# Attention and a max-out feed-forward layer on one core: the first q and k on other queues, another order in batch 0, and another way to sum the last 64 queries

## The chip, the cores and the metric

The kernel runs on one core of a Trainium2 chip. The metric is the time of one execution on the device in microseconds (us); a kernel is run several times and the median is given. A core has five engines that run at the same time and wait for one another through semaphores: PE (matrix multiplication; its weight loads are listed as PEld), DVE (vector), ACT (scalar functions such as exp), POOL (general purpose) and SP (issues transfers). ACT and POOL issue transfers as well. SBUF is the working memory with 128 partitions; PSUM is the small memory that PE writes to and that DVE and ACT empty. Each engine runs its instructions in the order of the program.

## The reference

Attention on 8 batches of 12 heads, 448 queries and keys, 64 values a head, with 1 added to the softmax's sum ("off by one"), and then a feed-forward layer whose hidden value is the maximum of three products:

```
scores = scale * q @ k.T                       # 8 x 12 heads, 448 x 448, d = 64
m = max(scores);  e = exp(scores - m)
attn = e / (sum(e) + exp(-m) + 1e-09)
x = (attn @ v) as tokens x 768                 # 3584 tokens, 12 heads x 64
h = max(x @ w1, x @ w2, x @ w3)                # 768 x 768 each
out = h @ w_out                                # 3584 x 768, fp32
```

Inputs and output are fp32. The kernel computes its products in fp16 and takes exp without subtracting the maximum, so the denominator is the sum of exponentials plus 1.

## The kernel before, in words

**Groups.** Four heads of one batch make a group: 24 groups, three a batch. A pair (`pr` 0 or 1) is two heads of a group. A group's q and k come as `ld_q` and `ld_k`, v as `ld_v`, all cast to fp16 by POOL's transfers (`load_qk`, L113; `load_v`, L123 and L126; weights `load_weight`, L137). There are four buffers of each kind. Of groups 0 and 1 q and k are loaded pair by pair.

**Scores.** q and k must lie with the head's 64 values on partitions. For groups 0 to 6 PE transposes them into PSUM tiles `trT` (`transpose_pe`, L205, for groups 0 to 2; `transpose_once`, L221, for 3 to 6) and ACT or DVE copies them to `KT` and `QT` (`evac`, L180 or L182); later groups use transposing transfers on SP (L233), and POOL completes `QT` (`shift_q`, L241). `scores` (L296) multiplies 64x64 blocks of k with all query columns into PSUM tiles `stp`; ACT takes the exponential into `e` (L316). The blocks are worked in seven units, 0 to 6.

**Sums of values.** For each pair `av_tail` (L336) adds the block of keys that both heads share a tile for, with 64*64 matmuls, and `av_main` (L353) the rest, with 128*128 matmuls: the weights are 128 queries of `e`, the moving data are 64 values and a column of constants that gives the sum of exponentials. Both write a tile `avp` of the same PSUM pool (`ps_s`, 3 buffers) as `stp`. 448 queries are worked as four windows of 128, of which the last holds only 64 that count. DVE then adds the 1 (`rb`, L363), takes the reciprocal (L366) and multiplies (`xn`, L369). `xn` is transposed to `xT`, by PE for batches 0 and 1 (`x_transpose_pe`, L396; `x_transpose_all`, L409), then by SP's transfers (L419).

**Feed-forward.** `up_piece` (L436) multiplies one of the three weights with `xT` into a PSUM tile `p_i`: six matmuls of 448 columns a piece, or twelve where a batch's columns are cut into even and odd queries. DVE copies the first weight's product to `hT` (L445) and takes the maximum for the others (L447). `out_piece` (L460) multiplies with `w_out` into `op_ps`, six matmuls, DVE scales it into `o_sb` (L467), SP stores it (L477). `p_i`, `op_ps` and most transposes share the PSUM pool `ps_b`, which has two buffers.

**Order.** The order is written out by hand. The program's first part takes groups 0 to 2 (batch 0) in two passes, first three of seven query columns ("O"), then four ("E"), so that PE has work while loads arrive; `warm` runs matmuls on zeros. Then the loop `for i in range(3, NI)` makes three visits a group: the scores of two, two and three units, in the first two visits the sums of the group before, and then `fill`, which takes pieces of feed-forward work from a list until a credit of columns is used up. In a visit PE thus runs scores (8 or 12 matmuls), a sum (16 + 24), and usually two or three pieces.

Window `w` of block `n` starts in `e` at

```
n * S + ((192, 320, 0, 128) if n % 2 == 0 else (0, 128, 256, 384))[w]
```

Of the kernel before, what the change touches and what calls it, by code (L numbers as in the profile page):

```python
# [21 lines left out]
def kernel(  # L22
# [33 lines left out]
    PE_QK = 7  # L56
    NF = 3
    PE_X = 2
    NEB = 2
    NV = 3  # L60

    tabs = list(get_activation_tables(nc.m.arch).keys())
    act_set = tabs.index("natural_log_exp_and_others")
    nc.scalar.add_instruction(
        mybir.InstLoadActFuncSet(
            name=nc.get_next_instruction_name(),
            act_func_set_id=act_set,
            ins=[],
            outs=[],
        )  # L70
    )

    cpool = ctx.enter_context(tc.tile_pool(name="const", bufs=1))
    att_pool = ctx.enter_context(tc.tile_pool(name="att", bufs=3))
    small = ctx.enter_context(tc.tile_pool(name="small", bufs=3))
    xn_pool = ctx.enter_context(tc.tile_pool(name="xn", bufs=3))
    xt_pool = ctx.enter_context(tc.tile_pool(name="xt", bufs=3))
    ht_pool = ctx.enter_context(tc.tile_pool(name="ht", bufs=2))
    out_pool = ctx.enter_context(tc.tile_pool(name="outp", bufs=3))

    ps_s = ctx.enter_context(tc.tile_pool(name="ps_s", bufs=3, space=bass.MemoryType.PSUM))
    ps_b = ctx.enter_context(tc.tile_pool(name="ps_b", bufs=2, space=bass.MemoryType.PSUM))
# [56 lines left out]

    wz = cpool.tile([128, 512], MMDT, name="wz")  # L140
    nc.vector.memset(wz, 0.0)
    load_qk(0, "kq", (0, 1))
    load_qk(0, "kq", (1, 2))
    ident16 = cpool.tile([128, 128], MMDT, name="ident16")
    make_identity(nc, ident16)
    load_qk(1, "kq", (0, 1))
    load_qk(1, "kq", (1, 2))
    load_v(0)
    load_qk(2)
    load_v(1)  # L150
# [8 lines left out]
    for j in range(NEB):  # L159
        nc.vector.memset(e_buf[j][:, NB * S : NB * S + HP], 0.0)  # L160
        blk = e_buf[j][:, 0 : NB * S].rearrange("p (n s) -> p n s", s=2 * S)
        nc.vector.memset(blk[:, :, NO : NO + HP], 0.0)

    def warm(n, cols=512):
        ps = ps_b.tile([128, 512], FP32, tag="b", name="warm")
# [152 lines left out]
    def e_col(n, w):  # L318

        return n * S + ((192, 320, 0, 128) if n % 2 == 0 else (0, 128, 256, 384))[w]  # L320
# [21 lines left out]
                        skip_group_check=True,  # L342
                    )

    def av_main(i, ej, pr, ws=(0, 1, 2, 3)):
        eF, vx = e_buf[ej], v_buf[i % NV]
        ps = avs.pop((i, pr))
        nw = len(ws)
        for hh in range(2):
            for j, w in enumerate(ws):  # L350
                for c, x in enumerate((X1, X3, X2)):
                    o = e_col(where[pr, hh, x], w)
                    nc.tensor.matmul(  # L353
                        out=ps[:, hh, j * D1 : (j + 1) * D1],
                        lhsT=eF[:, o : o + 128],
                        rhs=vx[:, 2 * pr + hh, (x[0]), 0:D1],
                        start=False,
                        stop=(c == 2),
                        skip_group_check=True,
                    )  # L360
        acc = ps[:, :, 0 : nw * D1].rearrange("p h (j d) -> p h j d", d=D1)
        rb = small.tile([P, 2, 4], FP32, tag="rb", name="rb")
        nc.vector.tensor_scalar(  # L363
            out=rb[:, :, 0:nw], in0=acc[:, :, :, D], scalar1=1.0 / LAMBDA, scalar2=None, op0=ALU.add
        )
        nc.vector.reciprocal(out=rb[:, :, 0:nw], in_=rb[:, :, 0:nw])  # L366
        if i not in xn:
            xn[i] = xn_pool.tile([P, NP, 4, 2, D], MMDT, tag="xn", name="xn")
        nc.vector.tensor_tensor(  # L369
            out=xn[i][:, pr, ws[0] : ws[0] + nw].rearrange("p j h d -> p h j d"),  # L370
            in0=acc[:, :, :, 0:D],
            in1=rb[:, :, 0:nw].unsqueeze(3).to_broadcast([P, 2, nw, D]),
            op=ALU.mult,
        )

    def prep_v(i, eng):
        t = raw[i]["v"]
# [198 lines left out]
    for n in (4, 5):  # L576
        ej, part, g, pp, pg = n % NEB, "E", n - 3, "E", n - 4
        scores(g, ej, (0, 1), part)
        scores(g, ej, (2, 3), part)
        av(pg, 1 - ej, 0, pp)  # L580
        if n == 4:
            transpose_once(3, "q", AC)
        else:
            x_transpose_pe(0, "E")
        fill(STEP)
        scores(g, ej, (4, 5), part)
        scores(g, ej, (6,), part)
        av(pg, 1 - ej, 1, pp)
        if n == 4:
            transpose_once(3, "k", AC)  # L590
        fill(STEP)
        if n == 4:
            shift_q(3, PL)
            load_v(4)
            load_qk(5)
            load_weight(3)


    visits = ((0, 1), (2, 3), (4, 5, 6))
# [18 lines left out]
    for i in range(3, NI):  # L618
        ej, pj = (i + 1) % NEB, i % NEB
        first = i == 3  # L620
        if PE_QK <= i + 2 < NI:
            transpose_dma(i + 2)
        if first:
            load_v(i + 2)
        for vi, units in enumerate(visits):
            n = 3 * i + vi
            scores(i, ej, units)
            if i == 4 and vi == 0:
                prep_v(i, DV)
            if vi < 2:  # L630
                av(i - 1, pj, vi, "E" if first else "EO")
            if vi == 1 and i > 3 * PE_X:
                x_transpose_dma(i - 1)
            if n in adds:
                add_batch(adds[n])
            per = STEP if first and vi < 2 else share(n)
            if vi == 0 and first:
                x_transpose_pe(1, "E")
            if vi == 2 and first:
                x_transpose_pe(i - 1, "E")  # L640
                fill(per / 2)
# [61 lines left out]
```

## Time and profile before

The median of 11 runs is 343.56 us (342.79 to 344.65).

| | |
|---|---|
| profiled execution, its own time | 344.66 us |
| span from its first to its last instruction | 342.9 us |
| PE busy | 329.2 us (96%) |
| DVE busy | 187.5 us (55%) |
| ACT busy | 151.4 us (44%) |
| POOL busy | 148.3 us (43%) |
| granted PE clock | 0.999 |

The page gives busy times, the chain of work that ended last (followed back from the last instruction, at each step to what released it), groups of instructions by line with their mean duration and the idle time before them, and transfers. In a line of a group or of the timeline, `out<-in` are the program's names, sizes are partitions x elements, `xN` is how many instructions it stands for, and square brackets tell how long the engine stood idle before and what it waited for. Starts are in us from the span's start. A line of the waits gives us in total, how many times, and the longest one.

### The profile page before, as it was taken

To read this page: it belongs to the slowest core of one execution; us is meant where nothing else is said; L and a number is where in the kernel's file an instruction comes from. 1 tells how busy PE (TensorE), PEld (TensorE's weight loads), DVE (VectorE), ACT (ScalarE), POOL (GpSimd) and SP (SyncE) were. 2 spreads that over 40 slices of the span, in tenths; PEclk is the share of its full clock that TensorE was granted. 3 is DMA by queue.
4 is the path that set the end of the run, shared out by engine and by line. 5 is a ranking of instruction groups with operands and counts; after the bars stand their busy time and mean duration, and the time that the engine had idled before them with its cause. 6 is when DMAs were issued, how large, how long until landed. Compare 5 with 4: busy or idle time off the path is not lost.

```text
span 342.9 us, 9827 instructions
## 1 busy us (share of the span) xinstructions
PE 329.2 (96%) x4175; PEld 199.1 (58%) x4175; DVE 187.5 (55%) x407; ACT 151.4 (44%) x181; POOL 148.3 (43%) x265
## 2 busy tenths in 40 slices
PE   7788899999999999999999999999999999999994
PEld 3556788766556555556556655556556655565552
DVE  3463566655555556555556556555556555565553
ACT  2757667664554444453444444543444444200000
POOL 8495688593772445373372465272454000000000
PEclk9999999999999999999999999999999999999999
DMA  7999999799899999969989999979993550124006
GB/s 86 192 164 187 204 207 201 108 162 202 154 122 120 162 222 142 170 74 236 137 111 94 187 215 124 114 128 203 160 117 46 124 125 3 31 67 106 0 15 169
DMA packets 84844, 46.19 MB, mean 135 GB/s; under 512 B 53312, under 2 KB 81344, under 8 KB 84800
## 3 DMA queue, kind: packets, MB, share of 16 engines
q0 software_dynamic: 29440, 22.03, 50.5%
q1 hardware_dynamic: 55120, 23.37, 38.0%
q8 instruction: 32, 0.52, 0.6%
q10 hardware_dynamic: 240, 0.16, 0.2%
q14 instruction: 12, 0.10, 0.1%
HBM read 44.04 MB, written 11.01 MB: 161 GB/s over the span
## 4 chain that ended last, share of the span: by engine, by line
PE 86%; DMA 8%; POOL 3%; issue 1%; DVE 0%; POOLq 0%
PE p_i L436 46%; PE op_ps L460 16%; PE avp L353 11%; PE stp L296 10%; DMA w<-in_moe_w_dram 4%; DMA ld_v<-in_v_dram 2%; PE avp L336 2%; DMA ld_q<-in_q_dram 2%; POOL w L137 1%; POOL ld_k L113 1%; POOL ld_q L113 1%; PE trT L221 1%; PE xtp L409 0%; POOL vx L379 0%; POOL vt L382 0%
## 5 line engine op out<-in xcount | busy, mean ns | idle before, releaser
L316 ACT ACTIVATE e<-stp 128x896 f16<-128x896 f32 (+4 forms) x171 | 144.2, 903 | 138.7 <-PE stp L296 138.6
L436 PE MATMUL p_i<-xT,w 128*128 128x448 f16 (+2 forms) x972 | 173.8, 332 | 2.9 <-DMA w<-in_moe_w_dram 2.8
L436 PEld LDWEIGHTS <-w 128*128 128x128 f16 x972 | 89.8, 98 | 70.8 <-issue 4.8
L241 POOL COPY QT<-QT 64x384 f16<-64x384 f16 (+1 forms) x84 | 46.7, 556 | 97.5 <-DMA QT<-ld_q 74.1
L447 DVE TENSOR_TENSOR hT<-hT,p_i 128x448 f16<-128x448 f16 (+2 forms) x96 | 59.7, 621 | 48.2 <-PE p_i L436 48.0
L460 PE MATMUL op_ps<-w,hT 128*128 128x384 f16 (+2 forms) x342 | 58.1, 323 | 0.0
L296 PE MATMUL stp<-QT,KT 64*64 64x448 f16 (+2 forms) x756 | 47.6, 338 | 2.4 <-DVE QT L182 2.0
L353 PE MATMUL avp<-vx,e 128*128 128x65 f16 x1152 | 45.4, 193 | 0.0
L460 PEld LDWEIGHTS <-hT 128*128 128x128 f16 x342 | 32.1, 98 | 22.7 <-issue 2.0
L467 DVE TENSOR_SCALAR o_sb<-op_ps 128x384 f32<-128x384 f32 (+2 forms) x57 | 31.2, 549 | 24.0 <-PE op_ps L460 22.3
L445 DVE CAST hT<-p_i 128x448 f16<-128x448 f32 (+2 forms) x48 | 30.0, 625 | 22.3 <-PE p_i L436 22.2
L353 PEld LDWEIGHTS <-e 128*128 128x128 f16 x1152 | 38.8, 97 | 2.3
L369 DVE TENSOR_TENSOR xn<-avp,rb 128x512 f16<-128x512 f32 (+1 forms) x54 | 34.1, 632 | 1.9
L296 PEld LDWEIGHTS <-KT 64*64 64x64 f16 x756 | 15.6, 105 | 26.6 <-issue 22.4
L363 DVE TENSOR_SCALAR rb<-avp 128x8 f32<-128x8 f32 (+1 forms) x54 | 8.9, 165 | 40.3 <-PE avp L353 40.2
L379 POOL COPY vx<-ld_v 128x768 f16<-128x768 f16 x21 | 17.2, 819 | 7.0 <-DMA ld_v<-in_v_dram 4.0
L336 PEld LDWEIGHTS <-e 64*64 64x64 f16 x768 | 15.0, 107 | 8.2 <-issue 1.5
L113 POOL DMA_DIRECT2D ld_k<-in_k_dram x26 | 18.4, 709 | 1.9 <-PE stp L296 1.1
L113 POOL DMA_DIRECT2D ld_q<-in_q_dram x26 | 18.6, 715 | 1.4 <-DMA w<-in_moe_w_out_dram 0.9
L336 PE MATMUL avp<-vt,e 64*64 64x65 f16 x768 | 15.6, 193 | 1.0 <-ACT e L316 0.7
L126 POOL DMA_DIRECT2D ld_v<-in_v_dram x24 | 15.2, 634 | 3.0 <-DMA w<-in_moe_w_dram 2.4
L123 POOL DMA_DIRECT2D ld_v<-in_v_dram x24 | 15.0, 627 | 2.1 <-DMA w<-in_moe_w_dram 1.7
(41 smaller groups left out, 87.0 us busy)
## 6 DMA issues: line engine op xcount, KB each, us to landing
out_dram<-o_sb SPq DMA_DIRECT2D x54, 192.0 KB, 4.1
ld_v<-in_v_dram POOLq DMA_DIRECT2D x48, 128.0 KB, 5.0
ld_k<-in_k_dram POOLq DMA_DIRECT2D x22, 224.0 KB, 6.7
ld_q<-in_q_dram POOLq DMA_DIRECT2D x22, 224.0 KB, 7.6
w<-in_moe_w_dram POOLq DMA_DIRECT2D x9, 384.0 KB, 9.5
w<-in_moe_w_out_dram POOLq DMA_DIRECT2D x3, 384.0 KB, 8.4
ld_k<-in_k_dram POOLq DMA_DIRECT2D x4, 112.0 KB, 4.4
ld_q<-in_q_dram POOLq DMA_DIRECT2D x4, 112.0 KB, 4.8
```

What stands on the lines that cost most here:

```text
L113: nc.gpsimd.dma_start(out=tiles[nm][:, 1 : NP * T + 1].rearrange("x (r t) d -> x r (t d)", r=NP)[:, p0:p1], in_=src[:, p0:p1],)
L241: eng.tensor_copy(out=t[d0 : d0 + HP, o * 128 : (o + n) * 128], in_=t[s0 : s0 + HP, a * 128 : (a + n) * 128],)
L296: nc.tensor.matmul(out=stp[half * HP : half * HP + HP, par, j * qn : (j + 1) * qn], lhsT=k_block(i, pr, h2, x[half]), rhs=q_cols(i, pr, h2 ...
L316: nc.scalar.activation(out=dst, in_=src, func=AF.Exp, scale=scale)
L336: nc.tensor.matmul(out=ps[half * HP : half * HP + HP, hh, j * D1 : (j + 1) * D1], lhsT=eF[hh * HP : hh * HP + HP, o : o + HP], rhs=vt[hh * ...
L353: nc.tensor.matmul(out=ps[:, hh, j * D1 : (j + 1) * D1], lhsT=eF[:, o : o + 128], rhs=vx[:, 2 * pr + hh, (x[0]), 0:D1], start=False, stop= ...
L369: nc.vector.tensor_tensor(out=xn[i][:, pr, ws[0] : ws[0] + nw].rearrange("p j h d -> p h j d"), in0=acc[:, :, :, 0:D], in1=rb[:, :, 0:nw]. ...
L436: nc.tensor.matmul(out=p_i[:, j * qn : (j + 1) * qn], lhsT=w_sb[i][:, dc, ts(fc, 128)], rhs=xT[b][:, dc, q0 : q0 + qn], start=(dc == 0), s ...
L445: nc.vector.tensor_copy(out=dst, in_=src)
L447: nc.vector.tensor_tensor(out=dst, in0=dst, in1=src, op=ALU.max)
L460: nc.tensor.matmul(out=op_ps[:, 0:w], lhsT=hT[bp][:, fc, ts(t, 128)], rhs=wout_sb[:, fc, c : c + w], start=(fc == 0), stop=(fc == NFC - 1),)
L467: nc.vector.tensor_scalar(out=o_sb[:, c : c + w], in0=op_ps[:, 0:w], scalar1=1.0 / LAMBDA, scalar2=None, op0=ALU.mult,)
```

## The change

It has three parts.

1. The first pair of group 0 comes as fp32 by a transfer of k on SP's queue and one of q on ACT's, and is cast by DVE and ACT. POOL then loads the second pair, and group 1 in whole groups. The load of ACT's table stands after ACT's transfer. DVE sets the identity's tile to zero in POOL's place.
2. Batch 0's work is in another order: the score unit S01 goes ahead of the second pair's transposes, both pairs' transposes of groups 1 and 2 stand together, v of group 0 is prepared earlier, and group 3's transposes in this part are copied by DVE instead of ACT. The weight of POOL's first load is issued whole, ahead of both preparations of v. Of the odd columns only the first two weights are worked in this part; the third weight's follow after the even columns of the first two. (Weights have indices 0 to 2 in the code.)
3. For groups 6 to 23 (`i >= LAST`) the sums of the last window, which has 64 queries, are made by `av_last` with 64*64 matmuls, for both heads and both halves of the keys, into one 65-column strip of each of the tile's two banks: the partitions tell the heads apart. DVE adds the two banks and scales each head by an instruction of its own, in fp16 into `xn`. `xn` has three fixed buffers whose unused part is zeroed once.

The output pool has 6 buffers instead of 3.

```diff
+    LAST = 6
...
-    xn_pool = ctx.enter_context(tc.tile_pool(name="xn", bufs=3))
-    out_pool = ctx.enter_context(tc.tile_pool(name="outp", bufs=3))
+    out_pool = ctx.enter_context(tc.tile_pool(name="outp", bufs=6))
...
-    load_qk(0, "kq", (0, 1))
+    ident16 = cpool.tile([128, 128], MMDT, name="ident16")
+    nc.vector.memset(ident16, 0.0)
+    first = {}
+    for nm, src, eng in (("k", k, nc.sync), ("q", q, nc.scalar)):
+        first[nm] = cpool.tile([P, T, D], FP32, name="first_" + nm)
+        pair = src[0, 0:2].rearrange("h (x t) d -> (h x) (t d)", t=T)
+        eng.dma_start(out=first[nm].rearrange("x t d -> x (t d)"), in_=pair)
...
     load_qk(0, "kq", (1, 2))
-    ident16 = cpool.tile([128, 128], MMDT, name="ident16")
-    make_identity(nc, ident16)
-    load_qk(1, "kq", (0, 1))
-    load_qk(1, "kq", (1, 2))
+    make_identity(nc, ident16, nomemset=True)
+    load_qk(1)
...
+    xn_buf = [cpool.tile([P, NP, 4, 2, D], MMDT, name=f"xn{j}") for j in range(NV)]
+    for j in range(NV):
+        nc.vector.memset(xn_buf[j][HP:P, :, 3], 0.0)
...
+    def av_last(i, ej, pr):
+        eF, vx, vt = e_buf[ej], v_buf[i % NV], vt_buf[i % NV]
+        ps = avs[i, pr]
+
+        def tile_mm(r, hh, o, rhs, stop):
+            nc.tensor.matmul(
+                out=ps[hh * HP : hh * HP + HP, r, 3 * D1 : 4 * D1],
+                lhsT=eF[r * HP : r * HP + HP, o : o + HP],
+                rhs=rhs,
+                start=False,
+                stop=stop,
+                skip_group_check=True,
+            )
+
+        n = where[pr, None, TL]
+        for hh in range(2):
+            tile_mm(hh, hh, e_col(n, 3), vt[hh * HP : hh * HP + HP, pr, 0:D1], False)
+        for c, x in enumerate((X1, X3, X2)):
+            for r in range(2):
+                for hh in range(2):
+                    o = e_col(where[pr, hh, x], 3)
+                    rhs = vx[r * HP : r * HP + HP, 2 * pr + hh, x[0], 0:D1]
+                    tile_mm(r, hh, o, rhs, c == 2)
...
+        if last:
+            end = small.tile([P, D1], FP32, tag="end", name="end")
+            nc.vector.tensor_copy(out=end, in_=ps[:, 1, 3 * D1 : 4 * D1])
+            nc.vector.tensor_tensor(
+                out=end, in0=ps[:, 0, 3 * D1 : 4 * D1], in1=end, op=ALU.add
+            )
+            nc.vector.tensor_scalar(
+                out=rb_all[:, 2 * nw :], in0=end[:, D:], scalar1=1.0 / LAMBDA, scalar2=None,
+                op0=ALU.add,
+            )
+        rb_in = rb_all if last else rb_all[:, 0 : 2 * nw]
+        nc.vector.reciprocal(out=rb_in, in_=rb_in)
...
+        if last:
+            for hh in range(2):
+                h = slice(hh * HP, hh * HP + HP)
+                nc.vector.tensor_scalar(
+                    out=xn[i][0:HP, pr, 3, hh], in0=end[h, 0:D], scalar1=rb_all[h, 2 * nw :],
+                    scalar2=None, op0=ALU.mult,
+                )
...
     def av(i, ej, pr, part):
-        av_tail(i, ej, pr, PW[part])
-        av_main(i, ej, pr, PW[part])
-
-    load_weight(0, (0, 1))
+        if i >= LAST:
+            av_tail(i, ej, pr, (0, 1, 2))
+            av_last(i, ej, pr)
+            av_main(i, ej, pr, (0, 1, 2), True)
+        else:
+            av_tail(i, ej, pr, PW[part])
+            av_main(i, ej, pr, PW[part])
+
+    load_weight(0)
     prep_v(1, PL)
-    load_weight(0, (2,))
     prep_v(2, PL)
...
-    warm(10)
+    warm(8)
+    evac(DV, raw[0]["k"][:, 1 : T + 1], first["k"])
+    evac(AC, raw[0]["q"][:, 1 : T + 1], first["q"])
     transpose_pe(0, 0, ps_s, DV, (AC, DV))
+    attend("O", 0, S01)
     transpose_pe(0, 1, ps_b, DV, (DV,))
-    attend("O", 0, S01, S23, S46)
-    warm(5)
+    attend("O", 0, S23, S46)
+    warm(4)
     transpose_pe(1, 0, ps_b, AC, (DV,))
+    transpose_pe(1, 1, ps_s, AC, (DV,))
     load_qk(4)
     load_weight(2)
     load_v(3)
-    attend("O", 1, S01)
-    transpose_pe(1, 1, ps_b, AC, (DV,))
-    attend("O", 1, S23, S46)
     prep_v(0, DV)
-    attend("O", 1, ("v", 0, 0), ("v", 0, 1))
+    attend("O", 1, S01, S23, S46, ("v", 0, 0), ("v", 0, 1))
     transpose_pe(2, 0, ps_b, AC, (DV,))
-    attend("O", 2, S01)
-    transpose_pe(2, 1, ps_b, DV, (DV,))
-    attend("O", 2, ("v", 1, 0), S23)
+    transpose_pe(2, 1, ps_s, AC, (DV,))
+    attend("O", 2, S01, S23, S46)
     x_transpose_pe(0, "O")
-    attend("O", 2, S46, ("v", 1, 1), ("v", 2, 0))
+    attend("O", 2, ("v", 1, 0))
     attend("E", 0, S01)
+    attend("O", 2, ("v", 1, 1), ("v", 2, 0), ("v", 2, 1))
     x_transpose_pe(1, "O")
-    attend("E", 0, ("v", 2, 1), S23)
+    attend("E", 0, S23)
     x_transpose_pe(2, "O")
-    add_up(0, NE, NO, [(i, f) for i in range(3) for f in (0, 2, 4)])
+    add_up(0, NE, NO, [(i, f) for i in range(2) for f in (0, 2, 4)])
...
-                add_up(0, 0, NE, [(w, f) for w in range(3) for f in (0, 2, 4)])
+                for w, cols in ((0, (0, NE)), (1, (0, NE)), (2, (NE, NO)), (2, (0, NE))):
+                    add_up(0, *cols, [(w, f) for f in (0, 2, 4)])
```

The even columns of groups 1 and 2 were a loop of two rounds and are written out, with the work in the order that part 2 tells.

More of the change, by code (lines that the diff above doesn't have):

```diff
@@ L58 @@
     PE_X = 2
+    LAST = 6
     NEB = 2
     NV = 3
[L62 to L71, printed above, removed]
     cpool = ctx.enter_context(tc.tile_pool(name="const", bufs=1))
@@ L141 @@
     nc.vector.memset(wz, 0.0)
-    load_qk(0, "kq", (0, 1))
+    ident16 = cpool.tile([128, 128], MMDT, name="ident16")
[5 more added lines that the diff above has]
+        eng.dma_start(out=first[nm].rearrange("x t d -> x (t d)"), in_=pair)
+    tabs = list(get_activation_tables(nc.m.arch).keys())
+    act_set = tabs.index("natural_log_exp_and_others")
+    nc.scalar.add_instruction(
+        mybir.InstLoadActFuncSet(
+            name=nc.get_next_instruction_name(),
+            act_func_set_id=act_set,
+            ins=[],
+            outs=[],
+        )
+    )
     load_qk(0, "kq", (1, 2))
-    ident16 = cpool.tile([128, 128], MMDT, name="ident16")
-    make_identity(nc, ident16)
-    load_qk(1, "kq", (0, 1))
-    load_qk(1, "kq", (1, 2))
+    make_identity(nc, ident16, nomemset=True)
+    load_qk(1)
     load_v(0)
@@ L343, in av_tail, with av_main @@
                     )
-    def av_main(i, ej, pr, ws=(0, 1, 2, 3)):
+    def av_last(i, ej, pr):
[19 more added lines that the diff above has]
+                    tile_mm(r, hh, o, rhs, c == 2)
+    def av_main(i, ej, pr, ws=(0, 1, 2, 3), last=False):
         eF, vx = e_buf[ej], v_buf[i % NV]
@@ L361, in av_main @@
         acc = ps[:, :, 0 : nw * D1].rearrange("p h (j d) -> p h j d", d=D1)
-        rb = small.tile([P, 2, 4], FP32, tag="rb", name="rb")
+        rb_all = small.tile([P, 2 * nw + 1], FP32, tag=f"rb{nw}", name="rb")
+        rb = rb_all[:, 0 : 2 * nw].rearrange("p (h j) -> p h j", h=2)
         nc.vector.tensor_scalar(
-            out=rb[:, :, 0:nw], in0=acc[:, :, :, D], scalar1=1.0 / LAMBDA, scalar2=None, op0=ALU.add
+            out=rb, in0=acc[:, :, :, D], scalar1=1.0 / LAMBDA, scalar2=None, op0=ALU.add
         )
-        nc.vector.reciprocal(out=rb[:, :, 0:nw], in_=rb[:, :, 0:nw])
+        if last:
[7 more added lines that the diff above has]
+                op0=ALU.add,
+            )
+        rb_in = rb_all if last else rb_all[:, 0 : 2 * nw]
+        nc.vector.reciprocal(out=rb_in, in_=rb_in)
         if i not in xn:
-            xn[i] = xn_pool.tile([P, NP, 4, 2, D], MMDT, tag="xn", name="xn")
+            xn[i] = xn_buf[i % NV]
         nc.vector.tensor_tensor(
@@ L371, in av_main @@
             in0=acc[:, :, :, 0:D],
-            in1=rb[:, :, 0:nw].unsqueeze(3).to_broadcast([P, 2, nw, D]),
+            in1=rb.unsqueeze(3).to_broadcast([P, 2, nw, D]),
             op=ALU.mult,
         )
+        if last:
[4 more added lines that the diff above has]
+                    scalar2=None, op0=ALU.mult,
+                )
     def prep_v(i, eng):
@@ L574 @@
     fill(STEP)
[L576 to L596, printed above, removed]
+    attend("E", 1, S01)
+    av(0, 1, 0, "E")
+    transpose_once(3, "q", DV)
+    attend("E", 1, S23)
+    fill(STEP)
+    attend("E", 1, S46)
+    av(0, 1, 1, "E")
+    transpose_once(3, "k", DV)
+    shift_q(3, PL)
+    load_v(4)
+    load_qk(5)
+    load_weight(3)
+    attend("E", 2, S01)
+    av(1, 0, 0, "E")
+    x_transpose_pe(0, "E")
+    attend("E", 2, S23)
+    fill(STEP)
+    attend("E", 2, S46)
+    av(1, 0, 1, "E")
+    fill(STEP)
     visits = ((0, 1), (2, 3), (4, 5, 6))
```

## The prediction

> **What bounds the kernel now.** I read the page first: busy shares, then the chain that ended last.
>
> ```profile
> span 342.9 us, 9827 instructions
> PE 329.2 (96%) x4175; PEld 199.1 (58%) x4175; DVE 187.5 (55%) x407; ACT 151.4 (44%) x181; POOL 148.3 (43%) x265
> ...
> PE 86%; DMA 8%; POOL 3%; issue 1%; DVE 0%; POOLq 0%
> ```
>
> PE carries 86% of the chain; DMA and POOL hold the rest, all at the start. Next, PE's waits by stretch: 4 to 25 us, 25 to 60 us (after 60 us that view lists no wait of PE at all).
>
> ```profile
> PE stp L296 <- DVE QT L182: 2.0, 3, 0.9
> PE trT L205 <- DMA ld_k<-in_k_dram: 0.7, 1, 0.7
> PE avp L336 <- ACT e L316: 0.7, 1, 0.7
> ...
> PE p_i L436 <- DMA w<-in_moe_w_dram: 2.8, 3, 1.2
> ```
>
> So time can be won before 45 us by waiting less, and after that only by giving PE less work; anything that makes PE wait after 60 us is lost in full. The timeline of one steady visit shows how much room the other engines leave:
>
> ```profile
> 104.49 0.30 PE L336 MATMUL avp<-vt,e 64*64 64x65 f16 x16
> ...
> 104.72 0.92 PE L353 MATMUL avp<-vx,e 128*128 128x65 f16 x24
> ...
> 105.48 3.57 PE L436 MATMUL p_i<-xT,w 128*128 128x448 f16 x18
> 105.68 0.17 DVE L363 TENSOR_SCALAR rb<-avp 128x8 f32<-128x8 f32 x1 [0.86 <-PE avp L353]
> 105.88 0.20 DVE L366 RECIPROCAL rb<-rb 128x8 f32<-128x8 f32 x1
> 106.12 0.69 DVE L369 TENSOR_TENSOR xn<-avp,rb 128x512 f16<-128x512 f32 x1
> 106.82 0.62 DVE L445 CAST hT<-p_i 128x448 f16<-128x448 f32 x1
> ...
> 111.01 0.69 DVE L369 TENSOR_TENSOR xn<-avp,rb 128x512 f16<-128x512 f32 x1
> 111.62 0.55 DVE L467 TENSOR_SCALAR o_sb<-op_ps 128x384 f32<-128x384 f32 x1
> ```
>
> After each sum of values (16 + 24 matmuls) DVE runs rb, reciprocal, xn, and only then empties the first feed-forward piece. These pieces alternate between two PSUM buffers (ps_b), so PE's third piece cannot start until DVE has emptied the first.
>
> **What the Trainium skill says.** "TensorEngine Tiling (Array Packing)", PSUM Bottleneck: tiling makes TensorE faster but not the emptying of PSUM, which may become the bottleneck. Before, there is slack (below), so no run shows it yet. "TensorE: Matmul & The Clock Gate", Packing small matmuls: tiles at different rows and columns of the array run concurrently. The trace agrees: 16 matmuls of 64*64 take 104.49 to 104.72, 0.23 us with the change of mode at the end, and 24 of 128*128 take 0.76 us, 31.7 ns each. "VectorE: DVE Perf Modes", on the TRN2 errata: a vector instruction pays a fixed cost however small it is. The trace agrees: L363 with 8 elements takes 167 ns and L369 with 512 takes 691, so 158 ns fixed + 1.04 ns an element. "Trainium Kernel Development and Optimization", Key Constraints: transfers from all issuing queues share the same 16 DMA engines. The DMA view of the first 45 us has them 90% or more busy from about 4 us on, so the new queues start transfers earlier but don't add bandwidth.
>
> **Part A, the start.** Before, POOL issues the first k at 1.24 us and q at 1.92, they land near 4.7 and 5.0, and the first transposes run at 4.90. After, SP and ACT issue at about 0.9. No load by these queues is in the trace; their stores of 64 KB land in 2.5 us. Estimate: both tensors, 458 KB in fp32, land at 3.6 to 4.4. Then a cast: DVE 0.15 + 448 x 1.04 ns = 0.4 to 0.6 us, ACT 0.6 (ACT's 128x512 copy took 0.60). Transposes at 4.6, gain 0.3; bounds 0.6 earlier and 0.4 later. The second pair is now first in POOL's queue (minus two issues of 0.55 to 0.69 us), and unit S01 goes ahead of its transposes, so group 0's exponentials end near 10.0, not 10.6. Group 1 is loaded whole, at DMA rate until about 10.7; its transposes then run together, its scores come in one block, and its last exponential ends near 15.3 (before 15.7). Group 2: with k and q in by about 14.2, S23 no longer sits behind POOL's preparation of v (done at 19.17 before, near 17 after), but exponentials of 0.81 us each and three ps_s buffers pace the rest. I get the first feed-forward piece at 24.0 instead of 25.05: gain 1.05, bounds 0.3 and 1.8.
>
> Then the weights. A piece x12 that doesn't wait takes about 1.0 to 1.1 us (36.02 to 37.11); with the waits for w index 1 and 2 they took 31.77 to 34.79 and 40.27 to 42.63, together 3.3 us too long. After, index 2 is first used at the end of the next loop iteration (i = 4), some 15 us later and long after it landed at 41.9: 1.4 us gained. Index 1 is used about 1.2 us of work later, at 31.7; its last third landed at 34.0 before. POOL's three w1 (index 0) issues are no longer split by the v copies, which left the DMA engines half idle at 19 to 21 us, so it should land about 1.9 us earlier, 32.1: 1.9 us gained at best, 1.4 at worst. Part A in sum: 1.05 + 3.3 = **-4.3 us**, between -3 and -5.5. Moving the transposes' evacuations to DVE, and the longer output pool (3 to 6; DVE waited 1.6 us on output stores, PE never) cost and bring nothing while PE is the bound.
>
> **Part B, groups 6 to 23, 36 sums.** PE: 16 small + 24 large matmuls become 12 + 14 small and 18 large. Four small ones at different tile positions go as one step of about 31 ns. Before: 4 + 24 = 28 steps; after: 3 + 1 (the two tails) + 3 + 18 = 25. Three steps of 31.7 ns and no further change of mode: 0.095 us x 36 = **-3.4 us**.
>
> DVE, from the start of the rb instruction, dependent instructions 0.034 us apart (105.85 to 105.88), independent ones overlapping by 0.08 (111.01 + 0.69 to 111.62): rb of 6 elements 0.00 to 0.16; copy of 65 from PSUM, 0.158 + 0.068 = 0.226, ends 0.31; addition 0.34 to 0.57; one-element tensor_scalar 0.15, ends 0.76; reciprocal of 7, 0.20, ends 0.99; xn of 384, 0.158 + 0.40 = 0.56, from 1.02 to 1.58; then two 64x64 tensor_scalars from 1.50 on. The nearest rows for these, the vt copies of 64 partitions, take 0.17 to 0.24, and what follows them doesn't overlap. So the next evacuation starts at 1.70 (all overlap) to 1.95 (none); I take **1.87**. Before it was 1.05 to 1.1.
>
> The room: the third p_i piece would start 12 x 0.189 us after the first, which is 0.20 before rb starts: at 2.07. DVE's evacuation takes 0.62 and PE follows 0.05 later (as after L182 at 8.33), so it must start by 1.39. For op_ps pieces (6 x 0.163 us, evacuation 0.556) by 1.14; before, 1.05 just met it. Only sums with three or more pieces behind them, with no scores between, are hit. In the changed order these are 15 with p_i pieces, 5 with op_ps, 1 mixed (limit 1.24), and the last sum, whose chain also waits for the one before it (0.87 more). Stalls: 15 x 0.48 + 5 x 0.73 + 0.63 + 0.87 = **+12.3 us**. Nothing later makes that up, since PE waits for nothing else there. The 14 sums with two pieces behind them have scores (0.40 us) and more before the third: hidden.
>
> xn is complete 0.8 us later for the transposing DMA (4.2 us to landing), but is read three visits later: hidden. At the end the last transpose is issued at 302.58 and its first reader is at 309.4, with 2.6 us over, of which about 1.7 go.
>
> **Sum.** -4.3 - 3.4 + 12.3 = +4.6 us against the profiled execution (span 342.9, its own time 344.66, so 1.8 around it and 1.1 above the median). I apply it to the median: 343.56 + 4.6 = 348.2, and put it at **348.0**.
>
> **Rivals.**
> - *The vector chain is hidden, and it is faster.* The stalls sum to 22 x offset - 28.8; they equal the 7.7 us gained at an offset of **1.66 us**. If the two narrow tensor_scalars and the one-element one cost 0.1 us each rather than 0.15 to 0.19, the offset is near 1.55, the stalls 5.3, the time 341.2. For: the small memsets follow one another in under 0.1 us. Against: every small instruction that reads data takes 0.16 or more. Chance 0.16.
> - *The start gives little.* DMA is full, and w index 1 is late again; a fp32 load in two queues takes bandwidth from the pair behind it. Gain 1.5 instead of 4.3: 351. Speaking against it: the wait on index 2 goes by order alone. Chance 0.16.
> - *The narrow tiles don't run four abreast.* In the new sums the two column halves of one row half take different moving data. If they serialise, 14 steps replace 4: 0.32 us x 36 = 11 us, time 358. Against: the score unit with the tails also has different moving data per half, and its 8 matmuls take the same 0.40 us. Chance 0.04.
> - *Forecast*, offset 1.75 to 1.95 and 3 to 5.5 at the start: 345 to 350.5. Chance 0.64.
>
> **How the numbers follow.** A difference under 0.2% (0.7 us) can't be told from none. Faster: most of the first rival, 0.13. Same: its edge and that of the forecast, 0.06. Slower: 0.81. The range 342.8 to 351.2 leaves out the fast half of the first rival and the third; the forecast's own is 345 to 350.5.
>
> **What would show it.** Waits of PE p_i and op_ps on DVE, absent now after 60 us, of 8 to 13 us in all, at the third piece after a sum; rb to next evacuation 1.8 to 1.9 us; DVE busy near 217 us; no wait of p_i on w over 0.5 us; the first piece near 24.0. Wrong if DVE's chain ends by 1.66, or if the start gains over 8 us.

## The result, and the profile after

The changed kernel takes **357.39 us** (median of 12 runs, 355.38 to 359.31) where the kernel before takes 343.43 beside it: 1.0403 times as long, with a 95% interval of 1.0385 to 1.0422. The profiled execution took 357.62 us against 344.66, its span (from the first to the last instruction) 355.8 against 342.9: **+12.9 us**, where +4.6 was forecast. The direction was right; the size was not, and the time lies above the range.

The page of the changed kernel, its span, busy times, the chain by engine, and one group of DVE instructions (how many | busy us, mean ns | idle before):

```profile
span 355.8 us, 10283 instructions
PE 330.1 (93%) x4316; PEld 196.4 (55%) x4316; DVE 220.2 (62%) x593; ACT 151.0 (42%) x181; POOL 146.4 (41%) x260
...
PE 71%; DVE 22%; issue 3%; ACT 2%; ACTq 0%; DVEq 0%
...
L425 DVE TENSOR_SCALAR xn<-end,rb 64x64 f16<-64x64 f32 x72 | 22.2, 308 | 0.5
```

DVE, at 0% of the chain before, now carries 22% of it; DMA and POOL are out of the chain. The two narrow scalings of each sum (L425) average 308 ns, more than the 0.17 to 0.24 us of the rows that the forecast took for them.

The waits of PE, first from 25 to 60 us, then from 60 us to the end (us in all, times, longest):

```profile
PE stp L304 <- ACT e L324: 0.6, 2, 0.4
...
PE p_i L490 <- DVE hT L501: 5.7, 9, 1.2
PE op_ps L514 <- DVE hT L501: 3.9, 4, 1.4
PE op_ps L514 <- DVE o_sb L521: 3.2, 5, 0.8
PE p_i L490 <- DVE hT L499: 2.8, 7, 0.7
```

The wait on weights is gone. After 60 us, where PE waited for nothing, it waits 15.6 us for DVE to empty feed-forward pieces: the place foreseen, but more than the 8 to 13 us named. The timeline of one visit with three pieces behind the sum shows the chain:

```profile
120.53 2.43 PE L490 MATMUL p_i<-xT,w 128*128 128x448 f16 x12
120.72 0.17 DVE L399 TENSOR_SCALAR rb<-avp 128x6 f32<-128x6 f32 x1 [0.84 <-PE avp L388]
120.81 0.22 DVE L404 COPY end<-avp 128x65 f32<-128x65 f32 x1
121.06 0.23 DVE L405 TENSOR_TENSOR end<-avp,end 128x65 f32<-128x65 f32 x1
121.32 0.15 DVE L408 TENSOR_SCALAR rb<-end 128x1 f32<-128x1 f32 x1
121.51 0.20 DVE L413 RECIPROCAL rb<-rb 128x7 f32<-128x7 f32 x1
121.74 0.56 DVE L416 TENSOR_TENSOR xn<-avp,rb 128x384 f16<-128x384 f32 x1
122.22 0.50 DVE L425 TENSOR_SCALAR xn<-end,rb 64x64 f16<-64x64 f32 x2
122.64 0.61 DVE L499 CAST hT<-p_i 128x448 f16<-128x448 f32 x1
...
123.30 0.54 PE L490 MATMUL p_i<-xT,w 128*128 128x448 f16 x2 [0.35 <-DVE hT L499]
```

From rb (120.72) to the emptying (122.64) it is 1.92 us. PE has filled both buffers of ps_b (12 matmuls) and starts the third piece only at 123.30. That is 0.51 us later than without a stall; the bracket counts only a part of it as idle, because the profile models the end of a matmul.

**Where the time went.** I read the start of the scores of iteration i = 7, just before the first sum of the new form, as a border: 79.54 us before, 75.86 after. The start thus gained 3.7 us. From there to the end it took 263.3 before and 279.9 after, 16.6 more. Between the first matmul of a sum and the first piece behind it there are 0.899 us on the mean instead of 0.990, which saves 0.091 x 36 = 3.3 us of PE's work. So PE stands still for 16.6 + 3.3 = **19.9 us**, where the forecast had 12.3.

### The profile page after: what moved, and what is told of

It is laid out like the page before. It is cut to its first block, busy times and chain, and to the rows that moved or that the text cites. A ratio compares the mean times of both kernels' runs of the same rounds, so it can differ in the third digit from the quotient of the medians.

```text
span 355.8 us, 10283 instructions
## 1 busy us (share of the span) xinstructions
PE 330.1 (93%) x4316; PEld 196.4 (55%) x4316; DVE 220.2 (62%) x593; ACT 151.0 (42%) x181; POOL 146.4 (41%) x260
## 4 chain that ended last, share of the span: by engine, by line
PE 71%; DVE 22%; issue 3%; ACT 2%; ACTq 0%; DVEq 0%
PE p_i L490 34%; PE op_ps L514 13%; PE stp L304 10%; PE avp L388 9%; DVE xn L425 5%; DVE xn L416 4%; DVE hT L501 3%; DVE rb L413 2%; DVE end L405 2%; ACT e L324 2%; PE avp L344 1%; DVE rb L399 1%; DVE rb L408 1%; PE warm L175 1%; PE avp L361 1%
## 5 line engine op out<-in xcount | busy, mean ns | idle before, releaser
L490 PE MATMUL p_i<-xT,w 128*128 128x448 f16 (+2 forms) x972 | 175.6, 332 | 8.8 <-DVE hT L501 5.7
L501 DVE TENSOR_TENSOR hT<-hT,p_i 128x448 f16<-128x448 f16 (+2 forms) x96 | 59.6, 621 | 37.6 <-PE p_i L490 34.9
L514 PE MATMUL op_ps<-w,hT 128*128 128x384 f16 (+2 forms) x342 | 59.1, 323 | 7.2 <-DVE hT L501 3.9
L388 PE MATMUL avp<-vx,e 128*128 128x65 f16 x936 | 38.6, 194 | 0.0
L388 PEld LDWEIGHTS <-e 128*128 128x128 f16 x936 | 32.1, 97 | 2.3
L416 DVE TENSOR_TENSOR xn<-avp,rb 128x384 f16<-128x384 f32 (+2 forms) x54 | 29.3, 543 | 2.1 <-DVE rb L413 0.2
L399 DVE TENSOR_SCALAR rb<-avp 128x6 f32<-128x6 f32 (+2 forms) x54 | 8.8, 164 | 34.1 <-PE avp L388 34.1
L425 DVE TENSOR_SCALAR xn<-end,rb 64x64 f16<-64x64 f32 x72 | 22.2, 308 | 0.5
L102 POOL DMA_DIRECT2D ld_k<-in_k_dram x24 | 17.4, 726 | 2.3 <-DMA w<-in_moe_w_out_dram 1.3
L102 POOL DMA_DIRECT2D ld_q<-in_q_dram x24 | 17.5, 730 | 2.1 <-DMA w<-in_moe_w_dram 1.1
L344 PEld LDWEIGHTS <-e 64*64 64x64 f16 x624 | 13.7, 107 | 7.9 <-issue 1.4
```

What stands on the lines that cost most here:

```text
L102: nc.gpsimd.dma_start(out=tiles[nm][:, 1 : NP * T + 1].rearrange("x (r t) d -> x r (t d)", r=NP)[:, p0:p1], in_=src[:, p0:p1],)
L388: nc.tensor.matmul(out=ps[:, hh, j * D1 : (j + 1) * D1], lhsT=eF[:, o : o + 128], rhs=vx[:, 2 * pr + hh, (x[0]), 0:D1], start=False, stop= ...
L416: nc.vector.tensor_tensor(out=xn[i][:, pr, ws[0] : ws[0] + nw].rearrange("p j h d -> p h j d"), in0=acc[:, :, :, 0:D], in1=rb.unsqueeze(3) ...
L425: nc.vector.tensor_scalar(out=xn[i][0:HP, pr, 3, hh], in0=end[h, 0:D], scalar1=rb_all[h, 2 * nw :], scalar2=None, op0=ALU.mult,)
L490: nc.tensor.matmul(out=p_i[:, j * qn : (j + 1) * qn], lhsT=w_sb[i][:, dc, ts(fc, 128)], rhs=xT[b][:, dc, q0 : q0 + qn], start=(dc == 0), s ...
L501: nc.vector.tensor_tensor(out=dst, in0=dst, in1=src, op=ALU.max)
```

## The experiments

The theory after this reading: the start gives most of what was forecast; PE's saving is real; the loss is DVE's longer chain between a sum and the next emptying, and it is larger than forecast because POOL's copies hold up the narrow scalings. Here is the place that suggested it, two visits of the changed kernel:

```profile
131.17 2.38 POOL L249 COPY QT<-QT 64x384 f16<-64x384 f16 x4 [1.97 <-DMA QT<-ld_q]
131.25 0.56 DVE L416 TENSOR_TENSOR xn<-avp,rb 128x384 f16<-128x384 f32 x1
131.73 1.33 DVE L425 TENSOR_SCALAR xn<-end,rb 64x64 f16<-64x64 f32 x2
...
135.42 0.74 POOL L102 DMA_DIRECT2D ld_q<-in_q_dram  x1
135.72 1.36 DVE L425 TENSOR_SCALAR xn<-end,rb 64x64 f16<-64x64 f32 x2
136.21 0.82 POOL L433 COPY vx<-ld_v 128x768 f16<-128x768 f16 x1
...
137.78 0.35 PE L490 MATMUL p_i<-xT,w 128*128 128x448 f16 x1 [0.96 <-DVE hT L501]
```

Two scalings take 1.33 and 1.36 us here instead of 0.50. The first time both stand beside copies on POOL; the second time the first of them stands beside POOL's issue of a transfer (459 ns) and the other beside a copy (883 ns). The second sum has only two pieces behind it, which the forecast called hidden; PE stands still all the same, after the next scores.

The runs were made in three lots, each beside the kernel before. In the table "rest" is from i = 7 to the end. Before and the three kernels that change the start alone take 263.3 to 264.0 there, about 263.5 (with the 263.3 of before alone, the changed kernel's stall is the 19.9 above). "Stall" is rest - 263.5 + 0.091 us for each sum in the new form. The rest holds 5.0 to 5.7 us behind the start of the last matmul, which differ from run to run, so stalls are good to some 0.5 us. From i = 7 to the start of the last matmul alone, before and the three take 258.3 to 258.4 us, the changed kernel 274.4, b_only 272.9, copies_act 271.2 and defer_act 255.3.

| | ratio to before (95%) | median us | i = 7 at | rest | stall |
|---|---|---|---|---|---|
| changed kernel | 1.0403 (1.0385 to 1.0422) | 357.39 | 75.86 | 279.9 | 19.7 |
| a_only | 0.9904 (0.9869 to 0.9939) | 341.00 | 75.50 | 263.6 | - |
| a_w2_early | 0.9920 (0.9899 to 0.9941) | 340.67 | 75.32 | 263.4 | - |
| a_pool_load | 0.9963 (0.9945 to 0.9981) | 342.75 | 76.94 | 264.0 | - |
| b_only | 1.0412 (1.0380 to 1.0443) | 357.25 | 76.94 | 278.1 | 17.9 |
| psum_end | 1.0427 (1.0381 to 1.0473) | 358.75 | 75.95 | 280.8 | 20.6 |
| copies_act | 1.0483 (1.0410 to 1.0556) | 359.20 | 80.91 | 276.7 | 16.5 |
| defer_narrow | 1.0003 (0.9985 to 1.0020) | 343.97 | 76.19 | 266.3 | 6.1 |
| defer_all | 0.9963 (0.9946 to 0.9980) | 342.52 | 76.19 | 263.7 | 3.5 |
| defer_tail | 0.9920 (0.9903 to 0.9937) | 340.59 | 75.76 | 262.4 | 2.0 |
| defer_act | 0.9838 (0.9797 to 0.9880) | 338.73 | 75.61 | 260.3 | -0.1 |

### a_only: the start without the new sums

```diff
-    LAST = 6
+    LAST = 99
```

> The changed kernel with the sums of all groups as before, so that only the start and the order of batch 0 are changed. If the two parts add up, the start is worth what the trace of the changed kernel shows at 76 us (the same scores began 3.7 us earlier): 339.7 us, and no wait of PE for DVE after 60 us. Rival: the start gave nothing that lasts, and all of the change's loss is somewhere in its first part: 343 us or more.

Measured: 341.00 us, 0.9904 times the time before, that is 2.1 to 4.5 us less by the interval; span 339.1. PE waits for nothing after 60 us, and the chain by engine reads

```profile
PE 93%; ACT 2%; DVE 2%; issue 1%; ACTq 0%
```

So parts 1 and 2 of the change win by themselves, somewhat less than forecast, and the whole loss comes with the new sums.

### b_only: the new sums without the start

The start is that of the kernel before; only part 3 of the change is in it (`av_last`, the `last` branch of `av_main`, the fixed `xn` buffers).

> Only the sums of the last 64 queries are changed; the start is that of before. If the parts add (theory): the changed kernel less the start's share, 357.4 + 2.7 to 3.8 = 360.1 to 361.2, with waits of PE on DVE after 60 us as in the changed kernel (15 to 16 us) and the waits on w back (about 3.3 us). Rival, that a later start meets the vector chain in another phase and hides some of its stalls: under 359.

Measured: 357.25 us, the same as the changed kernel. **The parts do not add**: alone the start wins some 3 us, with the new sums about nothing (1.0412 against 1.0403, each known to 0.2 or 0.3%). In the profiles the changed kernel is 1.1 us ahead at i = 7 and loses 1.8 in longer stalls (19.7 against 17.9; 1.6 of it before the last matmul). The time is the rival's, but most of the difference needs no other phase. Part 2 of the change also moves the third weight's pieces, and with them which pieces stand behind which sum. Ahead of the last pair, 18 sums have three pieces behind them in b_only (13 with p_i pieces, 5 with out pieces) and 20 in the changed kernel (14, 5 and a mixed one). The mixed one stalls for 0.9 us, and a sum with three p_i pieces for 0.5 to 0.6 where nothing disturbs: 1.4 to 1.5 us in all. The share of POOL is about the same in both (the scalings take 308 and 314 ns on the mean).

The profile of this run also says something on the forecast's first part. Its start has the order of the kernel before, yet i = 7 comes at 76.94 instead of 79.54, and of the waits on weights only this was left between 25 and 60 us:

```profile
PE p_i L486 <- DMA w<-in_moe_w_dram: 0.9, 1, 0.9
```

The last weight transfer of this part was issued at 25.5 us here, at 27.5 in the profile before. The 3.3 us of waits that the forecast counted as removable were thus partly that one execution's.

### a_w2_early: the start with the old order of the third weight

```diff
-    add_up(0, NE, NO, [(i, f) for i in range(2) for f in (0, 2, 4)])
+    add_up(0, NE, NO, [(i, f) for i in range(3) for f in (0, 2, 4)])
...
-                for w, cols in ((0, (0, NE)), (1, (0, NE)), (2, (NE, NO)), (2, (0, NE))):
-                    add_up(0, *cols, [(w, f) for f in (0, 2, 4)])
+                add_up(0, 0, NE, [(w, f) for w in range(3) for f in (0, 2, 4)])
```

> Only the start is changed, and of it the order is undone in which w2's odd columns go behind the even ones. Theory (this order removes the wait of the feed-forward pieces on w2): a wait on w2 of 2.8 us or more is back after 25 us and the time is 341.0 + 2.8 = 343.8, up to 346 as the pieces now come 2.5 us earlier. Rival (the earlier first pair alone brings the gain; ACT sets the pace of that stage anyway): 341.

Measured: 340.67 us, the time of the rival. The wait that this order was to remove is back with 0.4 us instead of 2.8 or more, and the time is that of a_only. Weights were issued up to 25.6 us here, as early as in b_only. Putting even queries ahead of w2 is worth nothing that can be measured. What does bring the gain this run does not tell; the next one does.

### a_pool_load: the start with the first pair on POOL's queue

```diff
-        eng.dma_start(out=first[nm].rearrange("x t d -> x (t d)"), in_=pair)
+    load_qk(0, "kq", (0, 1))
...
-    evac(DV, raw[0]["k"][:, 1 : T + 1], first["k"])
-    evac(AC, raw[0]["q"][:, 1 : T + 1], first["q"])
...
-    warm(8)
+    warm(10)
```

> Only the start is changed, and of it the fp32 loads of the first pair and their casts are undone: that pair comes by POOL's queue as before, the order of batch 0's attention stays the new one. Theory (the earlier first pair brings the start's gain): the first scores fall back from 6.2 to about 7.5 us, and 1.3 us of it reach the end: 341.0 + 1.3 = 342.3, up to 343.5 if all is lost. Rival (the order by arrival brings it): 341.0.

Measured: 342.75 us, in the range of the theory. Its first scores fell back by only 0.56 us (6.52, a_only 5.96), but the first scores of group 1 by 1.4 (12.12 against 10.69), and this lag is still there at i = 7 (1.4) and at the end (span 341.0 against 339.1). PE's wait ahead of group 1's transposes, at 10.84 us:

```profile
PE trT L209 <- DMA ld_q<-in_q_dram: 0.8, 1, 0.8
```

The fp32 loads bring about 1.9 us of span (1.8 between the medians, each measured in its own lot). The rest of the start brings the other 1.9 of span (342.9 to 341.0), but only 1.1 by the medians of this lot (343.81 to 342.75), since the time of before's profiled execution lay 1.1 us above the median.

### psum_end: the narrow instructions read PSUM

The sum of the two banks is written back to PSUM, so that the one-element addition and both scalings read PSUM instead of SBUF.

```diff
-            nc.vector.tensor_copy(out=end, in_=ps[:, 1, 3 * D1 : 4 * D1])
-            nc.vector.tensor_tensor(
-                out=end, in0=ps[:, 0, 3 * D1 : 4 * D1], in1=end, op=ALU.add
-            )
+            end = ps[:, 0, 3 * D1 : 4 * D1]
+            nc.vector.tensor_copy(out=tmp, in_=ps[:, 1, 3 * D1 : 4 * D1])
+            nc.vector.tensor_tensor(out=end, in0=end, in1=tmp, op=ALU.add)
```

> The changed kernel, but the sum of the two banks is written back to PSUM, so that the one-element and the two 64x64 instructions of DVE read PSUM instead of SBUF. Their number is the same. If the 64x64 instructions were long (0.31 us in the mean, up to 0.88) because they work in a mode that takes a port which POOL's copies hold, they now take 0.22 to 0.25 us throughout, rb to next evacuation is 1.9 us everywhere, and about 6.5 us are won: 351 us. Rival: POOL slows any vector instruction that runs beside it, or the long ones cost nothing: 356 to 358 us.

Measured: 358.75 us. No time was won, though the reason was half right. One line's instructions (ns: least, median, most), first of the changed kernel, then of this run:

```profile
L425 DVE TENSOR_SCALAR xn<-end,rb x72: 234/252/883, 78.9 to 315.1; 64x64 f16<-64x64 f32 x72
```

```profile
L424 DVE TENSOR_SCALAR xn<-avp,rb x72: 266/279/290, 79.0 to 315.9; 64x64 f16<-64x64 f32 x72
```

Reading PSUM, no scaling is held up any more, beside POOL's copies or not. The rival that POOL slows any vector instruction beside it is thus out: the 19 scalings that met a copy took 278 ns on the mean, the others 279. But each takes 0.03 us more and the instructions run together less, so the emptying came 2.10 or 2.17 us after rb in all but the last pair, instead of 1.91 or 2.03 with some up to 2.87. The run took the delay by POOL away and lengthened the chain; it could not say what the delay costs. The next one can.

### copies_act: POOL's copies on ACT

```diff
-            shift_q(i + 2, nc.gpsimd)
+            shift_q(i + 2, AC)
...
+            if vi == 1 and 5 <= i + 1 < NI:
+                prep_v(i + 1, AC)
...
-        if 5 <= i + 1 < NI:
-            prep_v(i + 1, nc.gpsimd)
```

> The changed kernel with the shifts of q and the copies of v that run beside the last sums (batches 1 to 7) moved from POOL to ACT; no vector instruction is changed. Theory (POOL's copies hold the port that the two 64x64 scalings need): no scaling over 0.27 us, next evacuation 1.9 us after the sum's first vector instruction everywhere, and 15 lengthened scalings x 0.25 us = 4 us less, about 353.5. Rival (the chain is long by itself, POOL has no part): 357. Rival (some 75 us more on ACT delay the exponentials): PE waits on ACT appear after 60 us and the time is over 358.

Measured: 359.20 us, by two effects that the trace keeps apart. No vector instruction was touched, and the scalings are even now:

```profile
L426 DVE TENSOR_SCALAR xn<-end,rb x72: 236/246/255, 83.9 to 316.9; 64x64 f16<-64x64 f32 x72
```

From i = 7 on it is 3.2 us shorter than the changed kernel (276.7 against 279.9). Forecast were 4. **So POOL costs 3 to 3.5 us of the stall**, and 16.5 us of it are the chain's own. This is POOL's whole share: in the changed kernel five scalings of 340 to 459 ns met no copy but an issue of a transfer by POOL, and in this run none was held up by an issue either. Ahead of i = 7, 67 us more on ACT in the whole kernel cost 5.0 us (80.91 against 75.86), as the second rival had it; PE waits there for ACT:

```profile
PE stp L305 <- ACT e L325: 1.0, 1, 1.0
PE p_i L491 <- ACT QT L188: 0.8, 1, 0.8
```

### defer_narrow: the two scalings behind the next emptying

The scalings and the transposing transfer that reads them are put in a list that is emptied behind the first emptying of a feed-forward piece (or ahead of the next sum). No work is left out.

```diff
+            def scale_end():
+                for hh in range(2):
+                    ...
+            late.append(scale_end)
...
+        flush()
...
-                x_transpose_dma(i - 1)
+                late.append(lambda j=i - 1: x_transpose_dma(j))
```

> The changed kernel with the two 64x64 instructions (and the transposing transfer that reads them) moved behind the first evacuation of a feed-forward piece after each sum. Nothing is left out. If PE waits because this evacuation comes later than 1.39 us (p_i) or 1.14 us (op_ps) after rb, it now comes at 1.49 and the waits shrink from 19 to about 4.5 us in all: 342 us. Rival: DVE has too much work in a visit as a whole, and the order of it makes no difference: 354 us or more.

Measured: 343.97 us, 13 less than the changed kernel, by moving instructions and taking none away. The emptying came 1.49 us after rb, and of the waits of PE after 60 us these were left:

```profile
PE op_ps L524 <- DVE hT L510: 1.6, 4, 0.8
PE op_ps L524 <- DVE o_sb L531: 1.1, 5, 0.4
```

The forecast's room was 1.39 us for p_i pieces and 1.14 for op_ps pieces. At 1.49 it gives 0.10 and 0.35; each stall was 0.09 and 0.34 (one emptying of 1.71 cost 0.56, and the room gives 0.57). This bears out the model of the stall: it is the offset, from rb to the emptying, less the room.

### defer_all: all six small instructions behind the next emptying

As defer_narrow, with the copy, the addition, the one-element addition and a reciprocal of its own in the same list.

> The changed kernel with all six instructions on the last 64 queries (copy, addition, one element, reciprocal, two 64x64) moved behind that evacuation. Nothing is left out. rb to evacuation is then 0.9 to 1.1 us, shorter than before the change, and PE's waits for DVE after 60 us are gone: the gain of the start (3.7) and of the matmuls (3.4) remains: 336.5 us. Rival (DVE's load as a whole): 350 us or more.

Measured: 342.52 us, less than before and after both. The emptying comes 0.97 to 1.14 us after rb, and most sums in the steady visits stall no more. It missed the expectation by 6 us. A stall of 1.8 us is left at the last two sums, which follow each other with no piece between, so that the second waits for the first one's list. Four others of 0.1 to 0.6 us, 1.2 in all, are gone in defer_act below, where the scalings leave DVE. The start of this execution was 0.7 us behind that of a_only, and the 3.7 us that the expectation took for the start are only 2.7 by the medians. The rest is open.

### defer_tail: the same, the last group in the old form

```diff
-        if i >= LAST:
+        if LAST <= i < NI - 1:
```

> The six small instructions of every changed sum behind the next evacuation as before, and the last group's two sums done in the old form. Theory: the stall of the last pair (1.9 us) goes, two sums cost 0.094 us each more: 342.5 - 1.9 + 0.2 = 340.8. Rival (the last pair's stall comes from the end of the work, not from the chain): 342.5.

Measured: 340.59 us; the last pair's stall of 1.8 us is gone. What was left are four waits of PE for DVE, 1.3 us in all.

### defer_act: and the two scalings on ACT

```diff
-                    nc.vector.tensor_scalar(
-                        out=xn[i][0:HP, pr, 3, hh], in0=end[h, 0:D], scalar1=re[h],
-                        scalar2=None, op0=ALU.mult,
+                    nc.scalar.activation(
+                        out=xn[i][0:HP, pr, 3, hh], in_=end[h, 0:D], func=AF.Copy, scale=re[h]
                     )
```

> The run with the last group in the old form, and the two 64x64 scalings of every changed sum on ACT, so that the port is not asked for. Theory (what is left of the stalls, 1.3 us on late evacuations, is scalings that POOL's copies lengthen): no wait of PE on DVE over 0.3 us after 60 us, 340.6 - 1.3 = 339.3. Rival (the scalings in ACT's queue hold up exponentials): 340.6 or more, with waits of PE on ACT after 60 us.

Measured: **338.73 us**, 0.9838 times the time before, and no wait of PE is listed after 60 us. This is the best of the kernels here. From i = 7 on PE's saving is there in full, behind the start of a_only (75.61 against 75.50). The span is 7.0 us shorter than before, the median 5.1; this profiled execution spent 2.9 us outside its span where that of before spent 1.8, and why is open. The timeline of a visit with three pieces:

```profile
117.35 3.38 PE L496 MATMUL p_i<-xT,w 128*128 128x448 f16 x17
...
117.97 0.56 DVE L409 TENSOR_TENSOR xn<-avp,rb 128x384 f16<-128x384 f32 x1
118.69 0.62 DVE L505 CAST hT<-p_i 128x448 f16<-128x448 f32 x1 [0.15 <-PE p_i L496]
119.23 0.22 DVE L420 COPY end<-avp 128x65 f32<-128x65 f32 x1
119.48 0.23 DVE L421 TENSOR_TENSOR end<-avp,end 128x65 f32<-128x65 f32 x1
...
120.12 0.70 ACT L430 ACTIVATE xn<-end,re 64x64 f16<-64x64 f32 x2 [1.85 <-DVE re L427]
```

DVE now waits 0.15 us for PE ahead of the emptying: the same work, with PE as the bound again. An exponential would have to be due in the 0.70 us of ACT's scalings to be late; ACT stood idle 1.85 us ahead of them.

## Why the prediction was wrong, step by step

| step | forecast | measured |
|---|---|---|
| first feed-forward piece at | 24.0 us | 22.49 us |
| start in all | -4.3 (-3 to -5.5) | -3.7 at i = 7 in the profiles; alone -2.7 in the medians |
| PE's work, 36 sums | -3.4 | -3.3 |
| rb to next emptying | 1.87 (1.70 to 1.95) | 1.91 to 2.03 undisturbed; up to 2.87 |
| stalls of PE | 12.3 | 19.9 |
| sum | +4.6 | +12.9 |

**PE's work was right**: 0.091 us a sum against 0.095, and defer_act shows it whole: from i = 7 to the last matmul 255.3 us against 258.4, 3.1 for its 34 sums. The rival that narrow tiles serialise is ruled out by this.

**The mechanism was right, the room too, and the offset nearly so where nothing disturbs.** The stall is the offset less the room (defer_narrow), and PE stands still at the third piece behind a sum, as foreseen. Undisturbed, the emptying starts 1.91 us after rb if it is a copy or a scaling, and 2.03, just beyond the forecast's 1.95, if it takes the maximum (L501).

**The step that failed is the size of the stalls** ("+12.3 us" in part B), by 7.6 us, and it has two halves.

- *The chain by itself: 16.5 instead of 12.3.* In copies_act, where POOL disturbs nothing, 14 sums with three p_i pieces stalled 7 x 0.51 + 7 x 0.63 = 8.0 us (15 x 0.48 = 7.2 forecast), five with out pieces 4.0 (3.65), the mixed one 0.9 (0.63), the last pair 1.5 (0.87), and two sums with one p_i and one out piece behind them 1.8; together 16.2 of the 16.5 us, and the rest lies behind the last matmul. The last two sums are of the 14 that the forecast called hidden behind the next scores; it was right for the 12 with two p_i pieces, as long as the offset was near 2. Of the 4.2 us too many, the two sums make 1.8 and the last pair 0.6; most of the others come from the offset, 1.91 and 2.03 instead of 1.87.
- *POOL: 3.4.* The forecast bounded a scaling by the copies of v on DVE, 0.17 to 0.24 us, and took that as the whole range. This is the bound that was wrong: 15 of the 72 overlap a POOL copy and take 0.49 us on the mean, 0.88 at most, so that offsets reach 2.87 us and sums with two p_i pieces stall as well (up to 1.0 us). Eleven of the 15 are longer than 0.3 us, and each of these ends 0.05 us after the copy that it met. Five more of the 72, which met no copy, are held up to within 0.02 us of the end of a transfer's issue on POOL. The trace of before had a sign of it that I did not use: a copy of v on DVE that takes 0.17 us alone takes 0.37 beside such an issue.

```profile
48.04 0.72 POOL L113 DMA_DIRECT2D ld_q<-in_q_dram  x1
48.40 0.37 DVE L381 COPY vt<-ld_v 64x128 f16<-64x128 f16 x1
```

The Trainium skill says why in "SBUF — State Buffer", Who interferes with whom: copies, casts and tensor_scalars between SBUF operands can take a second pair of ports that VectorE shares with GpSimd, under an exclusive lock, and the loser waits for the whole instruction. The runs agree: from SBUF beside POOL 234 to 883 ns, from PSUM 266 to 290, from SBUF with the copies on ACT 236 to 255.

**The start was over-valued in one term and under-valued in another**, so that -3.7 lies near -4.3 partly by luck. The first piece came 2.6 us earlier, not 1.05. The 3.3 us of waits on weights were mostly not the change's to win: undoing the order of w2 costs nothing (a_w2_early), and the old start in another execution has 0.9 us of them (b_only). Some 1.7 us of the two gains together are gone by i = 7: 0.6 of them are PE's waits on ACT's exponentials near 39 us, and the rest is open. I took one profiled execution's waits for a property of the kernel, though its own time lay 1.1 us above the median.

**That the parts add was assumed, and is not so**: the start is worth some 3 us alone and about nothing in front of the new sums. Most of it is that the start's new order of pieces puts two more sums ahead of three pieces (b_only). The forecast counted its stalls in that order, so its sum does not suffer from this.

**Smaller slips.** The offset before was given as 1.05 to 1.1; the prediction's own lines show 1.14 for a p_i piece (105.68 to 106.82). Three p_i pieces stand behind 14 sums, not 15. For the rival with serialised tiles, 11 us on top of 348 are 359, not 358. None of them changes the outcome.

## What to carry to other kernels

Work put between a producer and the next emptying of a two-buffer pool costs its latency once the room of two buffers is used up, however idle the engine's share of busy time looks; first ask if it can stand behind the emptying. Here moving six instructions a few places turned 357.4 us into 342.5, keeping the last group's sums in the old form made it 340.6, and giving two of the six to the idle engine 338.7. And before a short instruction is priced from an undisturbed row, look in the trace at what the same kind takes beside the neighbour that shares its ports, and count that into the range.

## What was not expected of the hardware

- A 64x64 scaling from fp32 in SBUF to fp16 takes 234 ns at least on DVE, but 266 to 290 from PSUM. The difference of the least values, 32 ns, is about what 32 elements take at the prediction's 1.04 ns. "VectorE: DVE Perf Modes", Mode 2×_2P, says that from SBUF to SBUF both read ports stream one half each; this agrees with it, and with the lock.
- An issue of a transfer by POOL holds such a scaling up only if it is some way on. The five that were held up started 0.19 to 0.31 us after the issue; seven of the eight others beside an issue alone, which took 236 to 252 ns, started 0.02 to 0.11 us after it. From PSUM, none was held up by an issue (267 to 290 ns).
- The same scaling takes 346 ns on ACT (68 of them, defer_act), longer than on DVE, and costs nothing there.
- Two scalings of 64 partitions in a row start 0.25 us apart, 234 ns long: they do not overlap, where rb and the copy behind it, of 128 partitions, overlap by 0.08 us. The second scaling also reads from partition 64 on and the first from 0; no run here tells the two apart.
- An emptying that takes the maximum starts 0.12 us later behind a scaling than one that copies (2.03 against 1.91).
